# A kernel with a checked fast path: the runtime choice of path moved ahead of the last two evictions

## The chip, the cores and the metric

The kernel runs on one core of one Trainium2 chip. The metric is device time in microseconds (us), from the start to the end of one execution; lower is better. The engines of a core are named as the profile names them: PE (matrix products; PEld is its weight load), DVE (VectorE), ACT (ScalarE), POOL (GpSimd) and SP (SyncE, which here only issues DMA transfers). A letter q behind an engine's name (SPq, DVEq) means its instruction queue: loads of registers, branches, waits on semaphores and DMA issues, which the profile does not count as busy time.

## The reference

Two blocks one after the other, all in float32. The first is a gated recurrence over the sequence, for each of 4 batch entries and 8 heads of width 48; the second is a gated state-space block on its output.

```python
def _attn_ref(q, k, v, alpha):                 # each (4, 8, 768, 48)
    for t in range(S):
        state = alpha[:, :, t, :, None] * state + np.einsum('bhd,bhe->bhde', k[:, :, t], v[:, :, t])
        y[:, :, t] = np.einsum('bhd,bhde->bhe', q[:, :, t], state)

def _moe_ref(x, w_in, A_log, w_out):           # x: (4, 768, 384), made of y
    val, gate = np.split(x @ w_in, 2, axis=-1)  # 512 columns each
    for t in range(S):
        h = np.exp(A_log)[0] * h + val[:, t, :]
        ys[:, t, :] = h
    return (gate * sigmoid(gate) * ys) @ w_out  # (4, 768, 384)
```

## The kernel before

The kernel holds two complete programs. `fast` computes the recurrence with running products of alpha and their inverses, which is right only while those products stay within bounds; it also takes the float64 weights apart by a short way that holds for a range of values. While it computes, it collects evidence that the inputs were within these bounds. `general` makes no such assumption and is slower. The top function (from L1055) runs `fast` in full, then branches on a flag: where a check failed, `general` computes everything again and writes over the output. With the inputs of the reference all checks hold, so the body of the branch is never executed, but every engine has to pass the branch and jump over the code of `general`.

`fast` cuts the 768 steps of each of the 4 batch entries into groups of 256, so there are N = 12 groups, numbered n. A group has two chunks of 128 rows, c = 0 and 1. The order of all work in `fast` is written out by hand[...]. For each group, the recurrence part (`keys`, `scores`, `masks`, `values`, `carried`, `join`) is followed by the second block: `block(n, cc)` for cc = 0 to 3, and `output(n)`. `block` projects 128 of the 512 inner columns into a value half and a gate half on PE (`project`, L801), runs the scan over the value half on DVE (`hidden`, L809), takes Silu of the gate on ACT (`gate`, L816), and multiplies both on POOL into a tile `f` (L817).

`output(n)` (L824) multiplies `f` by `w_out`: for each of the two chunks, four products over cc add up in one PSUM bank. Each of these float32 products is two passes on PE in the profile. The three products with cc = 0 to 2 are issued first, chunk 0 and then chunk 1 (`part(range(split))`); `finish` then issues the product with cc = 3 for chunk 0 and for chunk 1. After that each chunk is copied from PSUM to a tile `o_sb` and written to the output by a DMA that SP issues (L842). ACT makes these copies (L839), except in the last group, where DVE does (L841).

[...] `st` has one (pool `ps_st`), the pool `ps` has the other seven. `mm()` (L395) hands out its banks 0, 1 and 6 in turn; the tiles of `output` come from there. `pair_of()` (L398) alternates between a tile over banks 2 and 3 and two tiles in banks 4 and 5, and serves the recurrence part.

The evidence is brought together in `check_end` (L564). In group n = 10 DVE reduces it to one number per partition, `okc`, 1 where all is well. In group n = 11, after `block(n, 0)`, PE multiplies `okc` by a column of ones (L581): the result is one number, the count of good partitions. DVE compares it with 127.5 (L583) and casts it into `flag`, one int32 (L584). Before `output(11)`, `nc.values_load` (L1049) has all five engines load `flag` into a register; each does so when its queue comes to it. The branch itself (L1058) lies behind all work of `fast`.

Where the queues pass the branch, an engine that skips `general` still brings the semaphores to the counts that `general` would have left: the queue of each engine waits for its own semaphore's count and raises it, and SP does so for eight semaphores of DMA transfers (these instructions have L1058 in the profile). At the end of the program (L1085) SP waits for a list of semaphores, two by two, and all engines meet in a barrier.

Of the kernel before, what the change touches and what calls it, by code (L numbers as in the profile page):

```python
# [10 lines left out]
FP32 = mybir.dt.float32  # L11
U8 = mybir.dt.uint8
U32 = mybir.dt.uint32
AF = mybir.ActivationFunctionType
# [4 lines left out]
def general(  # L19
# [7 lines left out]
    moe_A_log: bass.AP,  # L27
    moe_w_out: bass.AP,
    out: bass.AP,
):  # L30

# [6 lines left out]
    nc = tc.nc  # L40
    B, H, S, D = q.shape
    DM = H * D
    DI = moe_A_log.shape[0]
    C = 128
    G = 2
    GC = G * C
    NG = S // GC
# [4 lines left out]
    NI = DI // C  # L52
# [3 lines left out]
    PS = bass.MemoryType.PSUM  # L56

    def pool(name, bufs, **kw):
        return ctx.enter_context(tc.tile_pool(name=name, bufs=bufs, **kw))

    const = pool("const", 1)
    p2 = pool("p2", 2)
    p3 = pool("p3", 3)
    wst = pool("wst", 2)
    ps_sc = pool("ps_sc", 2, space=PS)
    ps_tp = pool("ps_tp", 1, space=PS)
    ps_mm = pool("ps_mm", 3, space=PS)

# [32 lines left out]
    w_out = const.tile([C, NI, DM], FP32, name="w_out")  # L101
# [183 lines left out]
    def ssm(n):  # L285
        b, g = divmod(n, NG)
        x_sb = xs.pop(n)

        xT = p2.tile([C, NK, GC], FP32, name="xT")
        for c in range(G):  # L290
            tp = ps_tp.tile([C, NK, C], FP32, tag="tp", name="tpx")
            for kk in range(NK):
                nc.tensor.transpose(tp[:, kk, :], x_sb[:, c, ds(kk * C, C)], ident)
            nc.scalar.activation(xT[:, :, ds(c * C, C)], tp, AF.Copy)
        yield


        f = p2.tile([C, NI, GC], FP32, name="f")
        for cc in range(NI):
            pj = ps_mm.tile([C, 2, GC], FP32, tag="mm", name="pj")  # L300
            for i in range(2):
                for kk in range(NK):
                    nc.tensor.matmul(pj[:, i, :], w_in[:, kk, ds(i * DI + cc * C, C)], xT[:, kk, :],
                                     start=(kk == 0), stop=(kk == NK - 1))
            hh = p2.tile([C, GC], FP32, tag=f"h{cc}", name="hh")
            nc.vector.tensor_tensor_scan(
                out=hh, data0=a_dec[:, cc:cc + 1].to_broadcast([C, GC]), data1=pj[:, 0, :],
                initial=prev_h[cc][:, GC - 1:GC] if g else 0.0, op0=ALU.mult, op1=ALU.add)
            prev_h[cc] = hh
            sg = p2.tile([C, GC], FP32, name="sg")  # L310
            nc.scalar.activation(sg, pj[:, 1, :], AF.Sigmoid)
            nc.vector.tensor_mul(sg, pj[:, 1, :], sg)
            nc.gpsimd.tensor_mul(f[:, cc, :], sg, hh)
            yield

        for c in range(G):
            o = ps_mm.tile([C, DM], FP32, tag="mm", name="o")
            for cc in range(NI):
                nc.tensor.matmul(o, f[:, cc, ds(c * C, C)], w_out[:, cc, :],
                                 start=(cc == 0), stop=(cc == NI - 1))  # L320
            o_sb = p3.tile([C, DM], FP32, name="o_sb")
            nc.scalar.activation(o_sb, o, AF.Copy)
            nc.sync.dma_start(out=out[b, ds(g * GC + c * C, C), :], in_=o_sb)
            yield

    for n in range(B * NG + 1):
# [11 lines left out]
I32 = mybir.dt.int32  # L338
# [8 lines left out]
def fast(  # L347
# [7 lines left out]
    moe_A_log: bass.AP,  # L355
    moe_w_out: bass.AP,
    out: bass.AP,
):

# [4 lines left out]
    nc = tc.nc  # L366
    B, H, S, D = q.shape
    DM = H * D
    DI = moe_A_log.shape[0]
    C = 128  # L370
    G = 2
    GC = G * C
    NG = S // GC
    N = B * NG
    NT = GC // 32
    NK = DM // C
    NI = DI // C
    R = D - 32
    PS = bass.MemoryType.PSUM
# [4 lines left out]
    const = pool("const", 1)  # L384
    p1 = pool("p1", 1)
    p2 = pool("p2", 2)
    p3 = pool("p3", 3)
# [4 lines left out]
    ps = pool("ps", 1, space=PS)  # L392
    next_mm, next_pair = itertools.cycle("016"), itertools.cycle((0, 1))

    def mm(*dims, b=None):  # L395
        return ps.tile([C, *dims], FP32, tag=f"b{b or next(next_mm)}", name="mm")

    def pair_of(*dims, dtype=FP32):  # L398
        if next(next_pair):
            return [ps.tile([C, *dims], dtype, tag=f"b{b}", name="pair") for b in (4, 5)]  # L400
        t = both()
        n = dims[0] * dims[1]
        return [t[:, i, 0:n].rearrange("p (x y) -> p x y", x=dims[0]).bitcast(dtype) for i in range(2)]
# [46 lines left out]
    w_out = const.tile([C, NI, DM], FP32, name="w_out")  # L450
# [15 lines left out]
    one = const.tile([C, 1], FP32, name="one")  # L466
# [3 lines left out]
    mask = const.tile([C, C], FP32, name="mask")  # L470
# [21 lines left out]
    wmin = const.tile([C, NI + NW], FP32, name="wmin")  # L492
    wmax = const.tile([C, NI + NW], FP32, name="wmax")
    ok = const.tile([C, 4], FP32, name="ok")
    flag = const.tile([1, 1], I32, name="flag")

    def constants():
        nc.vector.memset(first, FLOOR)
        make_identity(nc, ident)
        for name in "akq":  # L500
            nc.vector.memset(natural(name, 0)[:, :, :, D:64], 1.0)

        nc.gpsimd.memset(mask, 1.0)
        nc.gpsimd.affine_select(out=mask, in_=mask, compare_op=ALU.is_ge, fill=0.0, base=0,
                                channel_multiplier=-1, pattern=[[1, C]])
        for t in vs:
            nc.gpsimd.memset(t[:, :, :, D:64], 0.0)
        for name in "akq":
            nc.gpsimd.memset(natural(name, 1)[:, :, :, D:64], 1.0)
        for t, x in ((minus, -1.0), (start_p, FIRST_PRODUCT), (last, 0.0), (aT[:, 4 * GC:], 0.0), (one, 1.0)):  # L510
            nc.vector.memset(t, x)
        for m in range(2):
            for name in "akq":
                nc.gpsimd.memset(raw_bufs[m][name].rearrange("p h n -> p (h n)")[:, G * H * 64:], 1.0)
# [49 lines left out]
    def check_end():  # L564
        red = const.tile([C, 4], FP32, name="red")
        rok = const.tile([C, N * 4], FP32, name="rok")
        X = mybir.AxisListType.X
        nc.vector.tensor_scalar(out=rok, in0=ratio.rearrange("p n h -> p (n h)"), scalar1=LEAST_PRODUCT,
                                scalar2=None, op0=ALU.is_ge)
        nc.vector.tensor_reduce(out=red[:, 0:1], in_=rok, axis=X, op=ALU.min)  # L570
        nc.vector.tensor_reduce(out=red[:, 1:2], in_=above, axis=X, op=ALU.max)
        nc.vector.tensor_reduce(out=red[:, 2:3], in_=wmin, axis=X, op=ALU.min)
        nc.vector.tensor_reduce(out=red[:, 3:4], in_=wmax, axis=X, op=ALU.max)
        for i, (op, x) in enumerate(((ALU.is_ge, 1.0), (ALU.is_le, 0.0), (ALU.is_ge, LEAST_HI),
                                     (ALU.is_lt, END_HI))):
            nc.vector.tensor_scalar(out=ok[:, i:i + 1], in0=red[:, i:i + 1], scalar1=x, scalar2=None, op0=op)
        okc = const.tile([C, 1], FP32, name="okc")
        nc.vector.tensor_reduce(out=okc, in_=ok, axis=X, op=ALU.min)
        yield
        n_ok = st[0:1, 0, 0:1]  # L580
        nc.tensor.matmul(n_ok, okc, one, start=True, stop=True)  # L581
        fl = const.tile([1, 1], FP32, name="fl")
        nc.vector.tensor_scalar(out=fl, in0=n_ok, scalar1=C - 0.5, scalar2=None, op0=ALU.is_ge)  # L583
        nc.vector.tensor_copy(out=flag, in_=fl)  # L584


    Zs = {}
# [32 lines left out]
    ends = [start_p]  # L620
# [171 lines left out]
    fs = {}  # L792
# [30 lines left out]

    def output(n):  # L824
        b, g = divmod(n, NG)
        os = [mm(DM) for c in range(G)]

        def part(ccs):
            for c in range(G):
                for cc in ccs:  # L830
                    nc.tensor.matmul(os[c], fs[n][:, cc, ds(c * C, C)], w_out[:, cc, :],  # L831
                                     start=(cc == 0), stop=(cc == NI - 1))

        def finish():
            part(range(split, NI))
            for c in range(G):
                o_sb = p3.tile([C, DM], FP32, tag="o_sb", name="o_sb")
                if n < N - 1:
                    nc.scalar.activation(o_sb, os[c], AF.Copy)  # L839
                else:  # L840
                    nc.vector.tensor_copy(out=o_sb, in_=os[c])  # L841
                nc.sync.dma_start(out=out[b, ds(g * GC + c * C, C), :], in_=o_sb)  # L842

        split = NI - 1 if n else NI // 2
        part(range(split))
        return finish


# [65 lines left out]
    next(steps)  # L914
    masks_near(0, 1)

    k10, q10 = (ps.tile([C, 4, C], FP32, tag=f"b{b}", name="pair") for b in (4, 5))
    natural_qk(1, "q", 0, q10)
    q_sb = p1.tile([C, 4, C], FP32, tag="q_sb", name="q_sb")
    nc.scalar.activation(q_sb, q10, AF.Copy)  # L920
# [65 lines left out]
    for n in range(1, N):  # L986
# [60 lines left out]
            next(end)  # L1047
        if n == N - 1:
            value = nc.values_load(flag[0:1, 0:1], min_val=0, max_val=1)  # L1049
        output(n)()  # L1050
    return value


@with_exitstack
def kernel(ctx: ExitStack, tc: tile.TileContext, *args):  # L1055
    with tc.manual_schedule():
        good = fast(tc, *args)
    with tc.If(good <= 0):  # L1058
        general(tc, *args)


# [28 lines left out]
```

## Time and profile before

| what | us |
|---|---|
| median of 3 runs (lowest, highest) | 296.93 (295.17, 298.25) |
| the profiled execution, its own time | 295.08 |
| span of the profiled execution, first to last instruction | 293.4 |
| PE busy in that span | 281.5 |
| ACT, POOL busy | 100.3, 116.4 |
| DVE busy | 224.7 |

| stretch of the span, us | PE busy | DVE busy | ACT busy | POOL busy |
|---|---|---|---|---|
| 0 to 10 | 10.00 | 6.31 | 4.07 | 5.20 |
| 50 to 100 | 49.32 | 43.94 | 18.33 | 24.33 |
| 200 to 250 | 50.00 | 40.67 | 16.48 | 16.95 |
| 270 to 280 | 10.00 | 2.53 | 1.89 | 1.45 |
| 280 to 294 | 7.51 | 1.86 | 0.62 | 1.45 |

The second table gives the busy microseconds of four engines within each stretch. A page of the profile shows one execution; its span is 1.7 us shorter than the time of that same execution, since the time also holds what lies before the first and behind the last instruction.

### The profile page before, as it was taken

To read this page: it belongs to the slowest core of one execution; us is meant where nothing else is said; L and a number is where in the kernel's file an instruction comes from. 1 tells how busy PE (TensorE), PEld (TensorE's weight loads), DVE (VectorE), ACT (ScalarE), POOL (GpSimd) and SP (SyncE) were. 2 spreads that over 40 slices of the span, in tenths; PEclk is the share of its full clock that TensorE was granted. 3 is DMA by queue.
4 is the path that set the end of the run, shared out by engine and by line. 5 is a ranking of instruction groups with operands and counts; after the bars stand their busy time and mean duration, and the time that the engine had idled before them with its cause. 6 is when DMAs were issued, how large, how long until landed. Compare 5 with 4: busy or idle time off the path is not lost. (4 is left out here: it accounts for less than half of the span.)

```text
span 293.4 us, 6146 instructions
## 1 busy us (share of the span) xinstructions
PE 281.5 (96%) x2345; PEld 226.5 (77%) x2345; DVE 224.7 (77%) x277; ACT 100.3 (34%) x226; POOL 116.4 (40%) x116
## 2 busy tenths in 40 slices
PE   7699999999999999999999999999999999999992
PEld 6578877885886896886886886886886886886870
DVE  5998887899996799799699699699699695312211
ACT  2457634432432432432432431431531531431110
POOL 7138791374642612642613513542523423401110
PEclk9999999999999999999999999999999999999998
DMA  9999969999992991991991991891891401101101
GB/s 129 163 162 298 366 125 169 233 264 212 237 207 65 236 167 34 246 187 35 244 175 34 241 185 34 219 202 37 210 213 39 108 11 35 54 11 31 55 4 63
DMA packets 71231, 42.09 MB, mean 143 GB/s; under 512 B 47492, under 2 KB 70536, under 8 KB 71192
## 3 DMA queue, kind: packets, MB, share of 16 engines
q1 hardware_dynamic: 69760, 40.96, 67.3%
q0 software_dynamic: 384, 0.44, 0.7%
q8 instruction: 20, 0.33, 0.6%
q10 hardware_dynamic: 1048, 0.20, 0.4%
q14 instruction: 19, 0.16, 0.2%
HBM read 33.33 MB, written 4.72 MB: 130 GB/s over the span
## 5 line engine op out<-in xcount | busy, mean ns | idle before, releaser
L801 PE MATMUL mm<-xT,w_in 128*128 128x256 f32 x576 | 131.0, 383 | 0.0
L801 PEld LDWEIGHTS mm<-xT,w_in 128*128 128x128 f32 x576 | 107.4, 190 | 17.8 <-issue 1.9
L817 POOL TENSOR_TENSOR f<-sg,hh 128x256 f32<-128x256 f32 x48 | 62.0, 1291 | 94.9 <-DVE hh L809 45.7
L831 PE MATMUL mm<-w_out,f 128*128 128x384 f32 x192 | 64.6, 487 | 0.7 <-DVE hh L809 0.6
L730 POOL TENSOR_TENSOR A<-A,mask 128x512 f32<-128x512 f32 x24 | 30.1, 1271 | 66.7 <-ACT A L729 66.7
L831 PEld LDWEIGHTS mm<-w_out,f 128*128 128x128 f32 x192 | 36.2, 190 | 24.1 <-DVE hh L809 1.3
L816 ACT ACTIVATE sg<-mm 128x256 f32<-128x256 f32 x48 | 18.4, 383 | 91.6 <-PE mm L801 89.5
L809 DVE TENSOR_TENSOR_SCAN hh<-a_dec,hh,mm 128x256 f32<-128x256 f32 x32 | 23.2, 726 | 20.2 <-PE mm L801 20.1
L734 DVE TENSOR_TENSOR A<-pair,mask 128x512 f32<-128x512 f32 x24 | 16.1, 688 | 26.6 <-ACT A L729 16.9
L661 DVE TENSOR_TENSOR_SCAN prod<-aT,first 128x1024 f32<-128x1024 f32 x10 | 27.5, 2750 | 0.1
L682 DVE TENSOR_TENSOR_SCAN inv<-aT,last 128x1025 f32<-128x1025 f32 x10 | 25.5, 2548 | 0.3
L839 ACT ACTIVATE o_sb<-mm 128x384 f32<-128x384 f32 x22 | 10.8, 490 | 43.8 <-PE mm L831 43.8
L714 PE MATMUL pair<-Z 48*128 48x128 f32 x384 | 25.2, 279 | 0.5 <-DVE first L627 0.2
L714 PEld LDWEIGHTS pair<-Z 48*128 48x128 f32 x384 | 22.6, 187 | 2.9 <-issue 2.1
L745 PE MATMUL pair<-A,v 128*64 128x128 f32 x352 | 21.3, 274 | 0.0
L745 PEld LDWEIGHTS pair<-A,v 128*64 128x64 f32 x352 | 19.1, 137 | 0.0
L647 DVE STREAM_TRANSPOSE aT<-raw_a 128x1024 f32<-128x1024 f32 x9 | 18.4, 2042 | 0.8 <-DMA raw_a<-in_alpha_dram 0.8
L647 DVE STREAM_TRANSPOSE Z<-raw_q 128x1024 f32<-128x1024 f32 x9 | 18.2, 2020 | 0.0
L647 DVE STREAM_TRANSPOSE Z<-raw_k 128x1024 f32<-128x1024 f32 x9 | 18.2, 2020 | 0.0
L729 ACT ACTIVATE A<-pair 128x512 f32<-128x512 f32 x24 | 13.3, 596 | 6.5 <-PE pair L714 3.5
L766 PEld LDWEIGHTS st<-v,ktm 128*64 128x64 f32 x320 | 11.4, 137 | 3.5 <-issue 3.5
L618 ACT ACTIVATE junk<-raw_a,minus 128x1024 bf16<-128x1024 f32 (+1 forms) x12 | 13.1, 1091 | 0.1
(119 smaller groups left out, 252.1 us busy)
## 6 DMA issues: line engine op xcount, KB each, us to landing
raw_k<-in_k_dram SPq DMA_DIRECT2D x24, 192.0 KB, 5.3
raw_q<-in_q_dram SPq DMA_DIRECT2D x24, 192.0 KB, 6.4
v<-in_v_dram SPq DMA_DIRECT2D x24, 192.0 KB, 6.4
out_dram<-o_sb SPq DMA_DIRECT2D x24, 192.0 KB, 1.9
raw_a<-in_alpha_dram SPq DMA_DIRECT2D x23, 192.0 KB, 4.2
raw_a<-in_alpha_dram SPq DMA_DIRECT2D x18, 176.0 KB, 4.3
raw_k<-in_k_dram SPq DMA_DIRECT2D x18, 176.0 KB, 5.7
raw_q<-in_q_dram SPq DMA_DIRECT2D x18, 176.0 KB, 6.7
```

Source lines behind the costliest of these rows:

```text
L647: nc.vector.transpose(out=to.rearrange("p h (c j) -> p h j c", j=NT), in_=raw_bufs[m % NR][name].rearrange("p h (j d) -> p h j d", d=D)[:, ...
L661: nc.vector.tensor_tensor_scan(out=prod, data0=al, data1=first.rearrange("p h n -> p (h n)"), initial=0.0, op0=ALU.mult, op1=ALU.max)
L682: nc.vector.tensor_tensor_scan(out=inv[:, ::-1], data0=aT[:, ::-1], data1=lasts[:, 0:4 * GC + 1][:, ::-1], initial=0.0, op0=ALU.mult, op1= ...
L714: nc.tensor.matmul(sc[i][:, p, :], Z[rows, p, 1, cols], Z[rows, p, 0, cols], start=True, stop=True)
L730: nc.gpsimd.tensor_mul(A[:, 1], A[:, 1], mask_all())
L734: nc.vector.tensor_mul(A[:, 0], sc[0], mask_all())
L745: nc.tensor.matmul(ys[m][i][ds(64 * s, 64), e, ds(c * C, C)], v_sb[:, c, 2 * p + i, :], A[:, i, p, :], start=(c == 0 and e == 0), stop=Fal ...
L801: nc.tensor.matmul(pj, w_in[cc][vg][:, kk, :], xT[:, kk, :], start=(kk == 0), stop=(kk == NK - 1))
L809: nc.vector.tensor_tensor_scan(out=hh, data0=a_dec[:, cc:cc + 1].to_broadcast([C, GC]), data1=pv, initial=prev_h[cc][:, GC - 1:GC] if n % ...
L816: nc.scalar.activation(sg, pg, AF.Silu)
L817: return lambda: nc.gpsimd.tensor_mul(fs[n][:, cc, :], sg, hhs.pop((n, cc)))
L831: nc.tensor.matmul(os[c], fs[n][:, cc, ds(c * C, C)], w_out[:, cc, :], start=(cc == 0), stop=(cc == NI - 1))
```

## The change

The branch moves from behind the last two copies to ahead of them. `output(11)` now issues its products and returns its two PSUM tiles without copying them; then comes the branch; behind the branch, two tiles `ends` in SBUF, made before `fast` and handed to both programs, are to hold the last 256 rows of the output. Where `general` ran, it has put its own last rows into `ends`. Then DVE copies the PSUM tiles of `fast` into `ends`, but only where a mask `good` says so, and SP writes `ends` to the output. So the last two evictions serve both paths: their result is that of `fast` where `good` is 1 and that of `general` where it is 0.

What this needs:

- The mask must stand in all 128 partitions: the product of the check is turned round, with a 128x128 matrix of ones as weights and `okc` as the moving column, so that each partition gets the count. `flag`, `fl` and the new byte tile `good` have 128 partitions, and there is one more cast.
- The PSUM tiles of the last product must outlive `fast`: they come from a new pool `end_ps`, which holds banks 4 and 5. `pair_of` takes its two banks from there as well.
- `general` now has six banks, and its `ps_sc` pool one buffer for two.
- In the last group the products are issued in another order: chunk 0 with cc = 0, 1, 2, then chunk 1 with cc = 0, then chunk 0 with cc = 3, then chunk 1 with cc = 1, 2, 3.

```diff
@@ general: in the last group
+            if n == B * NG - 1:
+                nc.vector.tensor_copy(out=ends[c], in_=o)
+            else:
+                ...
@@ fast: constants and check_end
+        nc.gpsimd.memset(ones, 1.0)
...
-        n_ok = st[0:1, 0, 0:1]
-        nc.tensor.matmul(n_ok, okc, one, start=True, stop=True)
-        fl = const.tile([1, 1], FP32, name="fl")
+        n_ok = st[:, 0, 0:1]
+        nc.tensor.matmul(n_ok, ones, okc, start=True, stop=True)
+        fl = const.tile([C, 1], FP32, name="fl")
         nc.vector.tensor_scalar(out=fl, in0=n_ok, scalar1=C - 0.5, scalar2=None, op0=ALU.is_ge)
         nc.vector.tensor_copy(out=flag, in_=fl)
+        nc.vector.tensor_copy(out=good, in_=fl)
@@ fast: output
-                if n < N - 1:
-                    nc.scalar.activation(o_sb, os[c], AF.Copy)
-                else:
-                    nc.vector.tensor_copy(out=o_sb, in_=os[c])
+                nc.scalar.activation(o_sb, os[c], AF.Copy)
                 nc.sync.dma_start(out=out[b, ds(g * GC + c * C, C), :], in_=o_sb)
+        if n == N - 1:
+            os = [end_ps.tile([C, DM], FP32, tag=f"b{b}", name="o") for b in (4, 5)]
+            part(range(NI - 1), 0)
+            part(range(1), 1)
+            part(range(NI - 1, NI), 0)
+            part(range(1, NI), 1)
+            return os
@@ fast: its end
             value = nc.values_load(flag[0:1, 0:1], min_val=0, max_val=1)
+            return value, good, output(n)
         output(n)()
-    return value
@@ the top function
+    sb = ctx.enter_context(tc.tile_pool(name="end_sb", bufs=1))
+    ps = ctx.enter_context(tc.tile_pool(name="end_ps", bufs=1, space=bass.MemoryType.PSUM))
+    ends = [sb.tile([C, cols], FP32, name=f"end{c}") for c in range(2)]
     with tc.manual_schedule():
-        good = fast(tc, *args)
-    with tc.If(good <= 0):
-        general(tc, *args)
+        value, good, os = fast(tc, *args, sb, ps)
+    with tc.If(value <= 0):
+        general(tc, *args, ends)
+
+    with tc.manual_schedule():
+        for c, (o_sb, o) in enumerate(zip(ends, os)):
+            nc.vector.copy_predicated(out=o_sb, mask=good.to_broadcast([C, cols]), data=o)
+            nc.sync.dma_start(out=out[entries - 1, ds(rows + (c - 2) * C, C), :], in_=o_sb)
```

More of the change, by code (lines that the diff above doesn't have):

```diff
@@ L29, in general @@
     out: bass.AP,
+    ends,
 ):
@@ L64, in general @@
     wst = pool("wst", 2)
-    ps_sc = pool("ps_sc", 2, space=PS)
+    ps_sc = pool("ps_sc", 1, space=PS)
     ps_tp = pool("ps_tp", 1, space=PS)
@@ L320, in ssm @@
                                  start=(cc == 0), stop=(cc == NI - 1))
-            o_sb = p3.tile([C, DM], FP32, name="o_sb")
-            nc.scalar.activation(o_sb, o, AF.Copy)
-            nc.sync.dma_start(out=out[b, ds(g * GC + c * C, C), :], in_=o_sb)
+            if n == B * NG - 1:
+                nc.vector.tensor_copy(out=ends[c], in_=o)
+            else:
+                o_sb = p3.tile([C, DM], FP32, name="o_sb")
+                nc.scalar.activation(o_sb, o, AF.Copy)
+                nc.sync.dma_start(out=out[b, ds(g * GC + c * C, C), :], in_=o_sb)
             yield
@@ L357, in fast @@
     out: bass.AP,
+    end_sb,
+    end_ps,
 ):
@@ L399, in pair_of @@
         if next(next_pair):
-            return [ps.tile([C, *dims], dtype, tag=f"b{b}", name="pair") for b in (4, 5)]
+            return [end_ps.tile([C, *dims], dtype, tag=f"b{b}", name="pair") for b in (4, 5)]
         t = both()
@@ L494, in fast @@
     ok = const.tile([C, 4], FP32, name="ok")
-    flag = const.tile([1, 1], I32, name="flag")
+    ones = const.tile([C, C], FP32, name="ones")
+    flag = end_sb.tile([C, 1], I32, name="flag")
+    good = end_sb.tile([C, 1], U8, name="good")
     def constants():
@@ L825, in output, with part, finish @@
         b, g = divmod(n, NG)
-        os = [mm(DM) for c in range(G)]
-        def part(ccs):
-            for c in range(G):
[L830 to L835, printed above, removed]
+        if n < N - 1:
+            os = [mm(DM) for c in range(G)]
+        def part(ccs, c):
+            for cc in ccs:
+                nc.tensor.matmul(os[c], fs[n][:, cc, ds(c * C, C)], w_out[:, cc, :],
+                                 start=(cc == 0), stop=(cc == NI - 1))
+        def finish():
+            for c in range(G):
+                part(range(split, NI), c)
             for c in range(G):
                 o_sb = p3.tile([C, DM], FP32, tag="o_sb", name="o_sb")
-                if n < N - 1:
-                    nc.scalar.activation(o_sb, os[c], AF.Copy)
-                else:
-                    nc.vector.tensor_copy(out=o_sb, in_=os[c])
+                nc.scalar.activation(o_sb, os[c], AF.Copy)
                 nc.sync.dma_start(out=out[b, ds(g * GC + c * C, C), :], in_=o_sb)
+        if n == N - 1:
[5 more added lines that the diff above has]
+            return os
         split = NI - 1 if n else NI // 2
-        part(range(split))
+        for c in range(G):
+            part(range(split), c)
         return finish
@@ L915, in fast @@
     masks_near(0, 1)
-    k10, q10 = (ps.tile([C, 4, C], FP32, tag=f"b{b}", name="pair") for b in (4, 5))
+    k10, q10 = (end_ps.tile([C, 4, C], FP32, tag=f"b{b}", name="pair") for b in (4, 5))
     natural_qk(1, "q", 0, q10)
@@ L1049, in fast @@
             value = nc.values_load(flag[0:1, 0:1], min_val=0, max_val=1)
+            return value, good, output(n)
         output(n)()
-    return value
 @with_exitstack
 def kernel(ctx: ExitStack, tc: tile.TileContext, *args):
-    with tc.manual_schedule():
-        good = fast(tc, *args)
-    with tc.If(good <= 0):
-        general(tc, *args)
+    nc, out = tc.nc, args[-1]
+    entries, rows, cols = out.shape
+    C = 128
+    sb = ctx.enter_context(tc.tile_pool(name="end_sb", bufs=1))
+    ps = ctx.enter_context(tc.tile_pool(name="end_ps", bufs=1, space=bass.MemoryType.PSUM))
+    ends = [sb.tile([C, cols], FP32, name=f"end{c}") for c in range(2)]
+    with tc.manual_schedule():
+        value, good, os = fast(tc, *args, sb, ps)
[5 more added lines that the diff above has]
+            nc.sync.dma_start(out=out[entries - 1, ds(rows + (c - 2) * C, C), :], in_=o_sb)
 _INS = ['q', 'k', 'v', 'alpha', 'moe_w_in', 'moe_A_log', 'moe_w_out']
```

## The prediction

> **What bounds the kernel now.** I read the engine totals of the page first, then the chain of waits, then the end of the timeline, then branch, semaphore and DMA rows one by one.
>
> ```profile
> PE 281.5 (96%) x2345; PEld 226.5 (77%) x2345; DVE 224.7 (77%) x277; ACT 100.3 (34%) x226; POOL 116.4 (40%) x116
> ...
> DVE o_sb L841 0%
> ```
>
> PE is busy for 96% of the span, so only two sorts of edit can move the time: those that lengthen or shorten PE's own work, and those in the 5.9 us behind PE's last product. The chain of waits is no help: it names a single piece, the last copy, and cannot follow what comes after, for that is queue work. The timeline of the last stretch shows where PE stops:
>
> ```profile
> 282.18 5.32 PE L831 MATMUL mm<-w_out,f 128*128 128x384 f32 x16
> 282.90 0.72 POOL L817 TENSOR_TENSOR f<-sg,hh 128x256 f32<-128x256 f32 x1 [1.86 <-ACT sg L816]
> 286.90 1.26 DVE L841 COPY o_sb<-mm 128x384 f32<-128x384 f32 x2 [4.99 <-PE mm L831]
> ```
>
> PE ends at 287.50 (282.18 + 5.32), the second copy at 288.16 (286.90 + 1.26), and SP issues its DMA at 288.19. The span ends at 293.35, 5.2 us after that copy. What fills it is seen in the rows of the line of the branch (durations in ns, then first and last start):
>
> ```profile
> L1058 PEldq COMPARE_BRANCH  x1: 3738/3738/3738, 283.7 to 283.7; - x1
> L1058 DVEq COMPARE_BRANCH  x1: 72/72/72, 287.6 to 287.6; - x1
> L1058 SPq COMPARE_BRANCH  x1: 50/50/50, 288.6 to 288.6; - x1
> L1058 DVEq EVENT_SEMAPHORE  x1: 21/21/21, 291.1 to 291.1; - x1
> L1058 SPq EVENT_SEMAPHORE  x8: 17/17/17, 289.1 to 291.7; - x8
> ```
>
> DVE branches at 287.6, but its next instruction runs at 291.1: 3.4 us for the jump. SP takes 0.5 us for its jump, then stops behind its third semaphore: the next, that of the transfer before last, comes only at 291.31. The DMA view of 288.15 to 289.6 says why:
>
> ```profile
> q1 hardware_dynamic: 255, 0.36, 67.7%
> q8 instruction: 1, 0.02, 6.2%
> q14 instruction: 1, 0.01, 1.3%
> ...
> out_dram<-o_sb SPq DMA_DIRECT2D x1, 192.0 KB, 3.2
> ```
>
> Instruction fetches share the DMA engines with the output. The 24 output transfers of the page have a median of 1.9 us to landing; this last one took 3.2. Window sums show the straggling: traffic falls from 139 to 26 GB/s, and lasts until 291.
>
> ```profile
> 289.30:290.10 0.80, 0.00 (x0) 0.00 (x0) 0.00 (x0) 0.00 (x0) 0.00 (x0) 1.00 0.44 139
> 290.10:291.00 0.90, 0.00 (x0) 0.00 (x0) 0.00 (x0) 0.00 (x0) 0.00 (x0) 0.71 0.07 26
> ```
>
> In the trace's semaphore increments, 14 of the last transfer's 16 parts have landed by 290.07, one lands at 290.79 and one at 291.40. [...] Then comes SP's list:
>
> ```profile
> L1085 SPq EVENT_SEMAPHORE  x12: 28/28/28, 291.7 to 292.4; - x12
> ```
>
> From landing (291.40) to the end of this list (292.54) are 1.14 us, and the barrier takes 0.81 more, to 293.35.
>
> [...] 2.65 us from branch to next instruction on ACT (283.0 to 285.65), 2.7 on POOL, 3.7 on PE, 3.4 on DVE. [...] the trace has 558 for the copy. [...]
>
> **The change part by part.**
>
> 1. *The check's product* (ahead of PE's last 13 us, so any loss is full). Before, the two passes of L581 pushed the pitch of PE's starts out: 273.88 to 274.63 where two ordinary steps of 0.216 take 0.43, so it cost 0.32. With 128 weight columns a load takes 190 ns (L801) for 82 now, in two passes: 2 x 0.108 = +0.22 if exposed; if the constant weights load beneath the product before, two steps at the ordinary pitch cost 0.43, +0.11. A better overlap could save 0.1. I take +0.1, from -0.1 to +0.25.
> 2. *Checks on DVE, memset on POOL*: one cast (0.14, as L584) and 128 partitions for one. DVE's next scan starts at 275.98, over a microsecond later: 0. The memset of `ones` (0.2, as that of `mask`, L503) stands ahead of six memsets of 0.47 to 0.52 that end at 5.95; POOL's next work is at 13.7: 0.
> 3. *Order and banks of the last product*: the same 16 passes, no fewer. Before, the first product started without a gap, so the banks release no wait: 0. Chunk 0 is now complete after 10 passes rather than 14; the passes follow at 0.3225 us, so at 287.52 - 6 x 0.3225 = 285.59. Product 5 needs `f` of cc = 3, there at 283.63 (282.90 + 0.72), and starts at 282.18 + 8 x 0.3225 = 284.76: no stall.
> 4. *The branch on DVE* now follows the last scan and the load of `flag` (281.19 + 0.54), at about 281.9. The jump costs 2.65 to 3.5: DVE is back at 284.6 to 285.4, before chunk 0 is complete. To delay chunk 1's copy (287.52), it must be back later than 286.9, 5.0 us after the branch. Queued behind it are only the two copies, and behind those SP's two transfers. Cost 0, hidden by PE's products.
> 5. *The branch on SP*: after `flag`'s load at 274.84, thus near 275.8, ahead of two DMA issues. Its semaphores are those of transfers landed by 274.1, so it passes at once: 0. ACT, POOL and PE pass the branch where they did; PE's is still behind all its products, and nothing of the last copies is issued there.
> 6. *The copies*: two by predicate. Chunk 0's lies between 285.6 and 286.2, hidden. Chunk 1's starts at about 287.6 as now and is on the path. The trace has no such operation[...]. I take 0, up to +0.4.
> 7. *Landing*: chunk 1's DMA goes at 288.2 as now. Chunk 0's is issued near 286.2, not 287.49, and has landed by 288.1. DVE's and SP's fetches are gone from this stretch. A landing in 1.9 us would save 3.2 - 1.9 = 1.3. But the 16 KB fetch at 288.15 follows PE's return from its branch (283.69 + 3.74 = 287.42), which doesn't move. It should be over by 289.6; a share's eight packets of 0.065 us (trace) could start then and end at 290.1. I leave 0.2 for it: -1.1, from 0 to -1.35.
> 8. *SP's list*: the five L1058 waits behind the landing (0.43) go ahead of it, and so does whatever part of the L1085 list precedes the last transfer's semaphore. If it is in the list's middle, about four waits of 0.061 are left: 0.3 in place of 1.14. I take -0.85, from -0.5 to -1.1.
>
> Sum: +0.1 + 0 - 1.1 - 0.85 = **-1.85 us**. Against the profiled execution: a span of 291.5 for 293.35, a time of 293.2 for 295.08. That execution lies 1.85 under the median of 296.93; taken off the median, **295.1 us**.
>
> **The rivals.**
>
> A. *The sum as above*: 295.1, own range 294.3 to 295.9. Chance 0.46.
>
> B. *The collision stays*: term 7 is 0, because PE's fetch, or another after the merge, still sits on one DMA engine. For it speaks that PE's jump isn't moved[...]. +0.1 - 0.85: 296.2. Chance 0.16.
>
> C. *The copies wait for PE's passage*: a program that joins two paths could hold every later reader until PE has raised its semaphore, at 287.55. Then both copies follow it: 2 x 0.56 behind 287.65, DMA at 288.85 rather than 288.19. -1.85 + 0.65: 295.7. Against it: [...] no L1058 wait names another engine's semaphore. Chance 0.14.
>
> D. *Slower, through PE's jump*: the same wait as C, with a late return. The three chunk-1 products now stand behind the wait for `f`, so PE's queue may branch later than 283.7. With return at R the last DMA goes at R + 1.25; the gains of terms 7 and 8 less 0.1 are 1.85, so it decides at R = 288.19 + 1.85 - 1.25 = 288.8, 1.4 after today's 287.42. R = 290 gives +1.2: 298.1; with slow predicate copies +2.0. Chance 0.10.
>
> E. *More than the sum*: DVE's return at 291.1 is only 0.3 before the landing. In an execution whose fetch takes longer, the whole excess is in the time. If the 1.85 between profile and median is that, it goes too: 293.2. Chance 0.14. Nothing shown proves that it is.
>
> That the change doesn't do what it says means here that the early branch uncovers no work: then C.
>
> **How the numbers follow.** The likeliest is A, 295.1. I count 1% (2.97 us) as about what a measurement of this kernel can tell from no change; three runs of one kernel span 3.1. The range takes in E at its lower end and B and C with the upper cost of the predicate copy and some scatter at its upper: 293.2 to 297.0; D and the far half of E stay out. Faster by over 1% means below 293.96: most of E, the edge of A: 0.2. Slower by over 1%, above 299.9, needs D with the slow copy, or an unforeseen stall: 0.09. Within 1%: 0.71.
>
> **What would show it.** Term 4: DVE's branch near 282, its next queue instruction before 285.6. Term 6: the form of the predicate copies, 560 ns, the first near 285.6, the second right behind PE's end. Term 7: the last output DMA 1.9 to 2.1 us to landing. Term 8: few SP semaphore rows between that landing and the barrier. Term 1: PE's end at most 0.25 later. The prediction is wrong if the first copy starts only after PE has ended (C, D), if the last landing still takes 3 us (B), or if PE's stretch before 287 grows.

## The result and the profile after

The changed kernel takes 294.47 us (median of 9 runs, 292.84 to 294.95); the kernel before, measured beside it, 296.19 (9 runs, 294.97 to 298.25). The ratio is 0.9931 with a 95% interval of 0.9903 to 0.996: 0.7% faster, about 2 us. A second set of runs of the changed kernel gave 293.74 and 0.9929 (0.9903 to 0.9954). The first profiled execution took 293.39, with a span of 291.66 where it was 293.35: 1.69 less.

The totals of the page and its chain of waits (shares of the span), for the changed kernel:

```profile
PE 281.0 (96%) x2345; PEld 226.4 (78%) x2345; DVE 224.8 (77%) x278; ACT 100.4 (34%) x226; POOL 116.8 (40%) x117
...
PE 82%; DVE 9%; DMA 4%; issue 2%; SPq 1%; POOL 0%; DVEq 0%; POOLq 0%
```

PE's count of instructions is what it was; there is one more on DVE and one on POOL. The chain, which named only the last copy before, now runs through the whole kernel, and shows in one line that PE sets the time. Of the 1.69, 1.64 lie behind PE's end: from PE's last semaphore increment to the end of the span it was 5.83 and is 4.19. The rows of the branch (its line is now 1082), each with count, duration in ns, and first and last start:

```profile
L1082 SPq EVENT_SEMAPHORE  x8: 17/17/17, 276.2 to 276.8; - x8
...
L1082 DVEq COMPARE_BRANCH  x1: 72/72/72, 281.8 to 281.8; - x1
...
L1082 PEldq COMPARE_BRANCH  x1: 3938/3938/3938, 283.6 to 283.6; - x1
L1082 DVEq EVENT_SEMAPHORE  x1: 21/21/21, 284.9 to 284.9; - x1
...
L1082 PEldq EVENT_SEMAPHORE  x1: 51/51/51, 287.7 to 287.7; - x1
```

SP is through its eight semaphores at 276.8, not 291.7. DVE jumps at 281.8 and is back at 284.9: the same three microseconds, now beside PE's last products. The timeline of the same stretch (start, duration, instruction, idle time before it):

```profile
282.13 5.32 PE L843 MATMUL o<-w_out,f 128*128 128x384 f32 x16
...
285.55 0.59 DVE L1087 COPY_PREDICATED end<-good,o 128x384 f32<-128x384 uint8 x1 [3.70 <-PE o L843]
286.17 2.26 SPq L1088 DMA_DIRECT2D out_dram<-end  x2
287.49 0.58 DVE L1087 COPY_PREDICATED end<-good,o 128x384 f32<-128x384 uint8 x1 [1.35 <-PE o L843]
```

Both copies wait for PE and for nothing else. The first starts at 285.55, two microseconds before PE's queue comes back from its own jump (283.65 + 3.94 = 287.59). The last transfer is issued at 288.10, and the row of its line says how long the two took to land:

```profile
DMA to landing us min/median/max: 2.2/2.3/2.5
```

In the trace's semaphore increments, 15 of the last transfer's 16 parts have landed by 290.05 and one lands at 290.59. The window sums agree: the view shows no traffic behind 290.1, where there was some until 291.

```profile
289.30:290.10 0.80, 0.00 (x0) 0.00 (x0) 0.00 (x0) 0.00 (x0) 0.00 (x0) 1.00 0.32 102
290.10:291.00 0.90, 0.00 (x0) 0.00 (x0) 0.00 (x0) 0.00 (x0) 0.00 (x0) 1.00 0.00 0
```

SP's list at the end of the program (line 1114) is mostly done ahead of the landing: nine waits start before 289.4, three are left.

```profile
L1114 SPq EVENT_SEMAPHORE  x9: 28/28/28, 288.8 to 289.3; - x9
...
L1114 SPq EVENT_SEMAPHORE  x3: 28/28/28, 290.6 to 290.7; - x3
```

### The profile page after: what moved, and what is told of

The parts are those of the page before. It is cut to its first block, busy times and chain, and to the rows that moved or that the text cites. A ratio compares the mean times of both kernels' runs of the same rounds, so it can differ in the third digit from the quotient of the medians.

```text
span 291.7 us, 6147 instructions
## 1 busy us (share of the span) xinstructions
PE 281.0 (96%) x2345; PEld 226.4 (78%) x2345; DVE 224.8 (77%) x278; ACT 100.4 (34%) x226; POOL 116.8 (40%) x117
## 4 chain that ended last, share of the span: by engine, by line
PE 82%; DVE 9%; DMA 4%; issue 2%; SPq 1%; POOL 0%; DVEq 0%; POOLq 0%
PE mm L813 38%; PE mm L843 19%; PE pair L726 7%; PE pair L757 6%; PE st L778 3%; PE pair L768 3%; PE mm L716 3%; DMA raw_k<-in_k_dram 2%; PE o L843 2%; DMA raw_a<-in_alpha_dram 2%; SPq L429 1%; PE st L898 1%; DVE Z L619 1%; DVE pair L551 1%; DVE inv L651 1%
## 5 line engine op out<-in xcount | busy, mean ns | idle before, releaser
L843 PE MATMUL mm<-w_out,f 128*128 128x384 f32 x176 | 59.3, 487 | 0.8 <-DVE hh L821 0.7
L843 PEld LDWEIGHTS mm<-w_out,f 128*128 128x128 f32 x176 | 33.1, 190 | 22.4 <-DVE hh L821 1.4
```

## The experiments

The profiled executions differ by up to 1.5 us in when PE ends. Those differences have arisen by 69 us: DVE's eighth scan of `hidden` starts between 67.4 and 68.9, and from there to PE's end all 13 traces take 219.85 to 220.15. The chains that were read there (changed, branch behind both copies, before without the branch) hold loads of the inputs. Whether such a difference belongs to the kernel or to the execution is not shown: the two kernels that were traced twice repeat their PE end within 0.15. So the traces are compared by the **tail**, from PE's last semaphore increment to the end of the span, and by the landing times; the medians and ratios stand beside them.

| kernel | tail | last two transfers, us to landing | median | ratio to before (95%) |
|---|---|---|---|---|
| before | 5.83 | 3.45, 3.21 | 296.19 | |
| before, again | 5.76 | 3.28, 3.05 | 296.24 | 0.9988 (0.9963 to 1.0013) |
| changed | 4.19 | 2.17, 2.49 | 294.47 | 0.9931 (0.9903 to 0.996) |
| changed, again | 4.53 | 2.30, 2.83 | 293.74 | 0.9929 (0.9903 to 0.9954) |
| changed, branch behind both copies | 5.78 | 2.10, 2.86 | 295.44 | 0.9948 (0.9931 to 0.9964) |
| changed, branch between the copies | 5.12 | 2.51, 2.06 | 294.98 | 0.9943 (0.9925 to 0.9961) |
| changed, old order of products | 5.26 | 3.73, 3.55 | 294.63 | 0.9939 (0.992 to 0.9959) |
| before, new order of products | 5.70 | 2.00, 2.75 | 295.77 | 0.9969 (0.9952 to 0.9985) |
| before, new check | 6.11 | 3.73, 3.50 | 295.93 | 0.9984 (0.9955 to 1.0014) |
| changed, last transfer on ACT | 3.81 | 2.43, 2.09 | 294.03 | 0.9922 (0.9894 to 0.9949) |
| changed, both transfers on ACT | 4.12 | 2.02, 2.41 | 294.86 | 0.9949 (0.993 to 0.9968) |
| changed, no branch | 3.62 | 1.87, 1.87 | 293.83 | 0.991 (0.9878 to 0.9941) |
| before, no branch | 3.67 | 1.90, 1.88 | 293.80 | 0.9906 (0.9869 to 0.9942) |

**The place of the branch.** First, all of the change but the place (the run has a helper function, written out here; `general` then sends its own last rows, as before):

```diff
     with tc.manual_schedule():
         value, good, os = fast(tc, *args, sb, ps)
+        for c in (0, 1):
+            nc.vector.copy_predicated(out=ends[c], mask=good.to_broadcast([C, cols]), data=os[c])
+            nc.sync.dma_start(out=out[entries - 1, ds(rows + (c - 2) * C, C), :], in_=ends[c])
     with tc.If(value <= 0):
...
-    with tc.manual_schedule():
-        for c, (o_sb, o) in enumerate(zip(ends, os)):
...
```

> The changed kernel with both predicate copies and both output transfers put back ahead of the branch; new check, new order of products, own banks all stay. Theory (the place of the branch is the whole gain): the jumps and the waits at the branch return behind the last transfer, span about 293.2, 1.5 above the changed kernel's 291.66; DVE back from its jump near 291; last transfer about 3 us to landing; time about equal to the kernel before (ratio 0.997 to 1.001). Rival (order of the products and the new banks made the gain): time stays that of the changed kernel, ratio about 0.993, span about 291.7.

The span was 293.71, later than the expected 293.2 by about as much as PE ended later (287.93 for 287.47); the tail was 5.78, as before. The rows of the branch in this kernel show both waits back at the end:

```profile
L1090 SPq EVENT_SEMAPHORE  x8: 17/17/17, 289.4 to 292.0; - x8
...
L1090 DVEq COMPARE_BRANCH  x1: 72/72/72, 288.0 to 288.0; - x1
...
L1090 DVEq EVENT_SEMAPHORE  x1: 21/21/21, 290.9 to 290.9; - x1
```

So the trace bears out the theory: the tail's 1.25 to 1.6 come and go with the place of the branch. The times do not show it by themselves. The ratio of 0.9948 misses the expected 0.997 to 1.001: this kernel is still 0.5% faster than the one before, with the branch where it was, and its interval (0.9931 to 0.9964) overlaps that of the changed kernel (0.9903 to 0.996). So another part of the change may have an effect of its own in time. The trace doesn't show where: it was taken from an execution of 295.44, this kernel's median, and its tail is that of the kernel before.

Then the branch between the two evictions:

```diff
     with tc.manual_schedule():
         value, good, os = fast(tc, *args, sb, ps)
+        nc.vector.copy_predicated(out=ends[0], mask=good.to_broadcast([C, cols]), data=os[0])
+        nc.sync.dma_start(out=out[entries - 1, ds(rows - 2 * C, C), :], in_=ends[0])
     with tc.If(value <= 0):
...
-        for c, (o_sb, o) in enumerate(zip(ends, os)):
+        for c, (o_sb, o) in ((1, (ends[1], os[1])),):
...
```

> The changed kernel with the branch between the two evictions: chunk 0 is copied and sent ahead of it, chunk 1 behind it. Theory (the jump of DVE costs about 3.2 us and is free only while PE's products run beside it): DVE branches at about 285.7, is back at 288.8 to 289.0, so chunk 1's copy starts 1.3 to 1.5 later than in the changed kernel (287.49) and its transfer lands near 291.9; span 292.9 to 293.1, about as the kernel before less 0.3. Rival (the gain comes from SP alone, whose waits at the branch go ahead of the transfer): copy of chunk 1 at 287.5, span 291.7.

The timeline of this kernel, and then DVE's rows of the branch:

```profile
286.15 0.58 DVE L1083 COPY_PREDICATED end<-good,o 128x384 f32<-128x384 uint8 x1 [3.70 <-PE o L843]
...
289.41 0.58 DVE L1083 COPY_PREDICATED end<-good,o 128x384 f32<-128x384 uint8 x1 [2.67 <-DVEq L1090]
```

```profile
L1090 DVEq COMPARE_BRANCH  x1: 72/72/72, 286.2 to 286.2; - x1
L1090 DVEq EVENT_SEMAPHORE  x1: 21/21/21, 289.2 to 289.2; - x1
```

PE was done at 288.06, and the copy of chunk 1 had to wait for DVE's return at 289.2. Its start is 1.35 behind PE's end, where the changed kernel has 0.02. The span was 293.18, just over the expected 292.9 to 293.1, since PE ended 0.6 later than in the changed kernel. This is the price of the same jump when nothing covers it. The tail grew by less, 0.6 to 0.9 against the two traces of the changed kernel, since the late transfer, issued 0.21 behind the end of PE's fetch, landed in 2.06. The ratio, 0.9943, can't be told from the changed kernel's.

**The order of the products.** The changed kernel with the old order:

```diff
-            part(range(NI - 1), 0)
-            part(range(1), 1)
-            part(range(NI - 1, NI), 0)
-            part(range(1, NI), 1)
+            for ccs in (range(NI - 1), range(NI - 1, NI)):
+                for c in range(G):
+                    part(ccs, c)
```

> The changed kernel with the last products in the order of the kernel before (cc 0 to 2 of both chunks, then cc 3 of both), in the same two banks. Theory (order costs and brings nothing as long as chunk 0's copy is done when chunk 1 is): chunk 0's copy starts at 286.85 rather than 285.55 and ends at 287.44, just before chunk 1's at 287.49; span within 0.2 of 291.66 unless the two transfers, now 0.65 apart, delay each other, then up to +0.3. Rival (the earlier first transfer is a good part of the gain): span 292.2 or more.

The span was 292.70 and the tail 5.26, so the rival's number came true in the trace, not the theory's; the ratio, 0.9939, can't be told from the changed kernel's. The DMA view of 288.2 to 291.2 in this kernel:

```profile
q1 hardware_dynamic: 288, 0.39, 37.2%
q8 instruction: 1, 0.02, 3.3%
q14 instruction: 1, 0.01, 0.6%
...
out_dram<-end SPq DMA_DIRECT2D x1, 192.0 KB, 3.5
```

All 288 packets of both transfers fall in this stretch, and so does one 16 KB fetch (288.26, 1.56 us long). Fifteen parts of either transfer had landed by 290.03; the sixteenth landed at 291.16 and 291.62. With the new order fifteen parts of the first transfer had landed by 288.03, ahead of that fetch (288.33 in the changed kernel).

The same order alone, in the kernel before (the diff is the one above, the other way round):

> The kernel before with nothing but the new order of the last products (chunk 0 complete after 10 of 16 passes, its copy and transfer 1.3 earlier); branch behind, old check, old banks. Theory[...]: 1.0 to 1.6 faster than before, ratio about 0.995, as with the branch put back behind the copies in the changed kernel. Rival (the order does nothing; banks or check brought what that kernel gained): ratio 0.998 to 1.002.

Ratio 0.9969, interval 0.9952 to 0.9985: the order alone makes the kernel before some 0.3% faster. That is between the theory and the rival, and more than its tail shows (5.70 for 5.76 and 5.83). It may account for a good part of what the kernel with the branch behind kept.

Why does the tail hardly move, though the last transfer took 2.75 rather than 3.21? SP's waits behind the branch show it, in two stretches of the trace:

```profile
L1063 SPq EVENT_SEMAPHORE  x3: 17/17/17, 288.9 to 289.1; - x3
...
L1063 SPq EVENT_SEMAPHORE  x5: 17/17/17, 291.0 to 291.4; - x5
```

The fourth wait is for the first transfer, which had landed completely by 288.02, and the last transfer had landed by 290.76. SP went on only at 291.02, so it was held by something other than its semaphores. Between the two stretches an 8 KB fetch ends at 289.94. In the two traces of the kernel before and in the one with the new check, SP's stop also ends 1.1 to 1.2 behind such a fetch, as here. That SP waited for a fetch of its own next instructions is the author's guess; no run tests it. The early branch takes this stop off the end as well: in the changed kernel SP goes through its eight waits between 276.2 and 276.8, without it.

**The check.** The kernel before with the wider check only:

```diff
-        nc.tensor.matmul(n_ok, okc, one, start=True, stop=True)
-        fl = const.tile([1, 1], FP32, name="fl")
+        nc.tensor.matmul(n_ok, ones, okc, start=True, stop=True)
+        fl = const.tile([C, 1], FP32, name="fl")
```

> The kernel before with nothing but the check's product turned round: the 128x128 ones as weights, flag in 128 partitions. Theory: the step costs PE 0.22 rather than 0.32 (pitch of its starts 0.655 where it was 0.749), so -0.1, which the times can't show: ratio 0.998 to 1.001. Rival (the wider check moves something else, as the loads at the start): ratio below 0.997.

PE's starts were 0.655 apart around the check (274.345 to 275.000), as in the changed kernel (273.920 to 274.575), for 0.749 before. The time shows nothing, as expected. The rows of the check's loads and products:

```profile
L583 PEld LDWEIGHTS st<-okc,ones x2: 190/190/190, 274.3 to 274.6; 128*128 128x128 f32 x2
L583 PE MATMUL st<-okc,ones x2: 167/208/250, 274.6 to 274.6; 128*128 128x1 f32 x2
```

A full load of 190 ns is no loss: it starts 0.21 ahead of its product, beneath the one before. In the kernel before, weight load and product of the check started together, 0.31 behind the start of the product before. In both kernels the wait for DVE stands on the load; why the short load started so late isn't shown.

**What is left of the branch.** Without it and without the general path, in the changed kernel and in the one before:

```diff
-    with tc.If(value <= 0):
-        general(tc, *args, ends)
```

> The changed kernel without the branch and without the general path behind it (that path is left out). Theory (what is left of the branch in the changed kernel is only a fetch that delays one 16th of the last transfer by 0.5): last transfer 1.9 to 2.0 to landing, stretch from PE's end to the end of the span 3.6 to 3.8 where it is 4.2; 0.4 to 0.6 faster than the changed kernel, ratio to the kernel before 0.990 to 0.992. Rival (the jumps still cost in the open): 1 or more faster than the changed kernel, ratio 0.988 or less.

> The kernel before without the branch and without the general path (that path is left out). Theory (the jumps, their fetches and the waits at the branch are all that the change could win): both last transfers land in 1.9 to 2.0 though they leave 0.7 apart, stretch from PE's end 3.7 to 3.9 where it was 5.8, time as the changed kernel without the branch (293.8) plus 0 to 0.3: ratio 0.990 to 0.992. Rival (old order or banks cost by themselves, branch or not): last landing 2.5 or more, stretch 4.5 or more.

The DMA view of 281 to 292 of the changed kernel without a branch:

```profile
q1 hardware_dynamic: 288, 0.39, 9.8%
...
out_dram<-end SPq DMA_DIRECT2D x2, 192.0 KB, 1.9
```

No instruction fetch is left in this stretch, and both transfers land in 1.87. In the kernel before without a branch they leave 0.7 apart, as they always did there, and the row of their line reads:

```profile
DMA to landing us min/median/max: 1.9/1.9/1.9
```

So neither the old order nor the two transfers close together cost anything in the tail by themselves. In both traces the 16 KB fetch is gone with the branch, and the delay with it (1.87 to 1.90 to landing, where the changed kernel's last transfer took 2.49 and 2.83). Both tails are alike (3.62 and 3.67), and so are both times. That is the whole price of the branch: 2.2 of the 5.83 in the trace, and 0.9% of the time (interval 0.6 to 1.3%, from six runs of the kernel before without the branch), of which the change takes back 0.7%. Without the branch, then, the rest of the change brings nothing that these runs can tell.

**Whose fetch delays the last part.** In the changed kernel an 8 KB fetch started at 289.52, while the last transfer's late sixteenth was under way. Was it this fetch that made it late? The last transfer was moved to ACT:

```diff
-            nc.sync.dma_start(out=out[...], in_=o_sb)
+            engine = nc.scalar if c else nc.sync
+            engine.dma_start(out=out[...], in_=o_sb)
```

> The changed kernel with the last transfer issued by ACT rather than SP. In the changed kernel one 16th of the last transfer was 0.5 us late[...]. Theory (this fetch is SP's own, drawn in by the semaphore waits that SP runs through behind its last issue at 288.1): SP passes those waits earlier, the fetch moves ahead of 288, the last transfer lands in 1.9 to 2.0 us rather than 2.49, span 291.1 to 291.2. Rival (the fetch belongs to PE's or DVE's queue): it stays at 289.5 and the landing at 2.5, span 291.7.

The fetch at 289.5 was gone, the landing took 2.09 rather than the expected 1.9 to 2.0, and the tail was 3.81. So that fetch goes with the last issue on SP. With both transfers on ACT:

> The changed kernel with both last transfers issued by ACT. Theory (SP's own fetch was what made one 16th of the last transfer late; with no issue left, SP runs through its waits before the transfers start): last transfer 1.9 to 2.1 to landing, stretch from PE's end 3.7 to 3.85 as with the last one alone on ACT (3.81), 0.3 to 0.5 faster than the changed kernel in the same job. Rival (that run was scatter): stretch 4.1 or more, same time as the changed kernel.

It was gone again, but the landing took 2.41 and the tail was 4.12: the theory failed, and the rival's numbers came true. The DMA view of 287.9 to 290.3 shows the one fetch left, which started at 288.00 and lasted 1.26:

```profile
q8 instruction: 1, 0.02, 3.3%
...
out_dram<-end ACTq DMA_DIRECT2D x1, 192.0 KB, 2.4
```

This is the one that follows PE's return, and the late part's landing goes with its end. The traces do not name the DMA engine of a packet, so which engine carried a fetch or a late part is not shown; what they show are the times. In each of the eleven traces with a branch there is one 16 KB fetch behind PE's return; in the two without, there is none. From its end to the landing of a late sixteenth it took (us):

| traces | first transfer's late part | last transfer's late part |
|---|---|---|
| old order of products (4) | 1.34 to 1.35 | 1.80 to 1.81 |
| new order, last transfer issued before the fetch ended (6) | landed before that end | 1.33 to 1.34 |
| branch between the copies: last transfer issued 0.21 after that end (1) | landed before that end | 2.28 |

The second row holds the traces with SP's fetch and both without it, so SP's fetch is not what made the last part late. With the old order the late parts of two transfers landed behind the fetch, 0.46 to 0.47 apart; with the new order only one did. That is what the order brings in the landing. How late the last part is then goes with the end of PE's fetch (289.26 and 289.50 in the two traces of the changed kernel, with 2.49 and 2.83 to landing). In time, both transfers on ACT gave 0.9949 where the changed kernel gave 0.9929 beside it, with overlapping intervals. No version with the branch is shown to be faster than the changed kernel.

**The kernels once more.**

> The kernel before once more, for a second trace of it and for the scatter of its own times. Its 56 runs so far have a median of 296.93, but its first profile came from a run of 295.08. Theory (a typical run loses another 1 to 2 us at the end, where instruction fetches meet the two output transfers, which leave 0.7 apart): stretch from PE's end to the span's end 6.5 to 7.5 in place of 5.83, one of the landings above 3.5. Rival (the difference lies in the loads of the first 75 us): PE's end 1 to 2 later than 287.5, stretch behind it 5.8. Ratio 0.998 to 1.002.

> The changed kernel once more, beside the next two on one chip. Theory (its gain is of the end alone): stretch from PE's end to the end of the span 4.1 to 4.4 as in its first trace (4.19), last transfer 2.2 to 2.6 to landing, ratio to the kernel before 0.991 to 0.995. Rival (the first trace was a lucky one, and a typical run keeps the collision): stretch 5 or more.

The second trace of the kernel before again came from an execution below its median (295.15 for 296.24), and its tail was the first one's: neither the theory nor the rival of that expectation was seen. What a typical run of the kernel before does in its other microsecond stays open. The second trace of the changed kernel had a tail of 4.53, its last landing 2.83 after issue: both are above the expected ranges and below the rival's 5. The end of PE's fetch was 0.24 later (289.50 for 289.26).

## Why the prediction was right, step by step

Predicted were -1.85 us and 295.1. The medians differ by 1.72, the first two profiled spans by 1.69, the spans of the second pair of traces by 1.52. The median itself, 294.47, is 0.6 below the predicted one: the prediction took its -1.85 off 296.93, and the kernel before measured 296.19 this time. The mechanism, early jumps and waits beside PE's products, is borne out; the closeness of the sum is in part luck, since term 7 fell short by 0.38 and PE's end, taken 0.1 later, came 0.05 earlier.

- *Term 1, the check's product*: taken at +0.1, measured -0.09 in the pitch of PE's starts. The full load runs beneath the product before; the prediction named that overlap as its lower end.
- *Term 2*: nothing, as said. DVE's extra cast took 0.148 at 274.79, long before its scan at 275.92.
- *Term 3, order and banks at nothing*: wrong as it stands. The order costs PE nothing (PE ended at 287.47 for 287.52), but with the old order two late parts landed behind PE's fetch and with the new one only one: a tail of 5.26 against 4.19 and 4.53. The prediction had this effect within term 7, where it let the first transfer land by 288.1 (fifteen of its parts did, the last at 288.34), so the sum was not hurt.
- *Term 4, DVE's jump*: branch at 281.75, back at 284.94, 3.19 for 2.65 to 3.5, and done before chunk 0 was complete at 285.53. The run with the branch between the copies shows the price without cover, 1.3.
- *Term 5, SP's jump*: branch at 275.74, all eight semaphores passed by 276.80. The prediction's reading of SP before was wrong, though: it took the stop until 291.31 as a wait for the transfer before last. That transfer had landed by 290.94, and with the new order of products in the kernel before SP stopped until 291.02 for a transfer landed at 288.02. The sum was not hurt, since SP's branch leaves the end either way.
- *Term 6, the copy by predicate*: 581 to 587 ns for 558. It costs within 0.03 us what the copy costs; the +0.4 allowed for was the author's estimate, which no trace had shown. It started 0.02 behind PE rather than 0.08, so the transfer left 0.63 after PE's end for 0.66 before.
- *Term 7, the landing*: taken at -1.1, measured -0.72 in the first pair of traces (3.21 to 2.49) and -0.22 in the second (3.05 to 2.83). It was the term mis-sized, though inside its range of 0 to -1.35. Right was that PE's fetch is what is left: it ran from 288.33 to 289.26 (288.15 to 289.59 in the kernel before), and the last part landed at 290.59. But the prediction's estimate took 0.5 from the end of that fetch to the end of the share, and the landing came 1.33 after it. SP's fetch at 289.5 makes no difference to that 1.33.
- *Term 8, SP's list*: taken at -0.85, measured -0.87 (from last landing to the span's end, 1.95 to 1.08).

The measured stretches add up, as they must: 0.05 from PE's earlier end, 0.03 from the copy, 0.72 and 0.87 make 1.67 of 1.69. The prediction's "3.7 us on PE" is the length of the branch's own record; PE's next instruction came 3.86 after the branch started, and 4.07 in the changed kernel.

Of the rivals, C and D are refuted by the trace: the first copy starts at 285.55, while PE's return is at 287.59. B came true in part, as the numbers of term 7 say: PE's fetch still ends 1.33 ahead of the last part's landing. E, a gain beyond the sum because typical runs lose more than the profiled one, is not seen in this comparison: the median of the changed kernel stands 1.1 above its profiled run, just as that of the kernel before does over nine runs (296.19 to 295.08).

Open is a part of the division in time. The traces give nearly all to the place of the branch; the times give 0.3% to the order alone (0.9969) and keep 0.5% with the branch behind, with intervals too wide to tell these kernels from the changed one or from each other. One trace of most kernels can't settle it. Nor did the prediction's first step name all the places where time can change: PE is also idle for some 6 us ahead of its last product (287.5 less 281.5), and the 1.5 us by which its end differs between traces have arisen by 69 us.

## What to carry to other kernels

Here the branch cost each engine its jump, from 0.5 us on SP to 3.86 on PE in the kernel before, and DVE's could be hidden: its 3.19 us beside PE's products cost nothing, while between the copies a jump of 3.0 us (286.2 to 289.2) made the second copy start 1.3 later. So let each engine pass the branch while another engine still has work that it must wait for anyway, and keep only what both paths share behind it. Look at what else comes with the jump. Behind the 16 KB fetch that follows PE's return, part of the last output landed late (2.49 and 2.83 after issue, for 1.87 without the branch), so get the early output out before that fetch (fifteen of its sixteen parts had landed by 288.03, the fetch started at 288.33), and judge the end by the last sixteenth of a transfer (290.59, where fifteen had landed by 290.05) rather than by its median. And before you put a stop down to a semaphore, check when that semaphore had come: SP's, of 291.02, had come at 288.02.

## What the runs showed of the hardware that was not expected

- A late sixteenth of a 192 KB transfer landed 1.33 to 1.35 after the end of the 16 KB fetch behind PE's return, in all ten traces where the transfer was issued before that end, and 0.46 to 0.47 later again for a second transfer; the other parts land mostly within 0.3 of each other. From issue to landing that made up to 3.73, where 1.87 to 1.90 were enough in the two traces without the branch. The fetch itself took 1.29 to 1.66 where both transfers were under way beside it, and 0.93 to 1.32 elsewhere.
- PE's return from the jump was followed by this further fetch 0.43 to 0.72 later (changed kernel: first instruction at 287.72, fetch at 288.33). DVE's return at 284.94 was followed by an 8 KB fetch at 285.53. What the jump itself waits for was not tested: the last fetch within PE's jump ended at 287.22, before the last transfer was issued (288.10); the one behind the return ended at 289.26, 1.33 ahead of the landing of the late part.
- A queue can stand still though its semaphore has come: SP passed its fourth wait at 291.02, three microseconds after the transfer had landed (kernel before with the new order).
- A product with a full set of constant weights and one moving column took 0.1 less of PE's pitch than one with a single, computed weight column and the constant column moving (0.655 for 0.749).
